# A second GpSimd drain near the end of the page stage, and two pages fewer turned on TensorE, in an attention and expert-routing kernel

## The chip, the cores and the metric

One core of one Trainium2 chip runs the whole program. The metric is the device time of an execution in microseconds (us). Several chips were used: times of one kernel on two of them differ by 1 to 2%, so only kernels timed on the same chip, in the same rounds, are compared.

## The reference, cut to what matters

The program computes random-feature attention over 8 batches, 8 heads, 576 positions, and sends its output through a mixture of 8 experts:

```python
x = attn_out.transpose(0, 2, 1, 3).reshape(B, S, H * D)     # 4608 tokens of 512
logits = x @ w_gate
e = argmax(logits) or the expert of the token before, by a local gate
h = maximum(x[b, s] @ w1[e], 0.0)                           # 512 -> 1024
out[b, s] = softmax(logits)[e] * (h @ w2[e])                # 1024 -> 512
```

The kernel sorts the tokens by expert into "pages" of 128 tokens, 18 pages for each half of the batch ("epoch 0" and "epoch 1") and 2 overflow pages that always run. A page is gathered from memory, turned (transposed), multiplied with its expert's first matrix, turned again, multiplied with the second, scaled, and scattered to the output rows.

## The kernel before: the parts that matter

NEP is 18. A page's step does three things: the hidden product of page j, the turning of the hidden tile of page j - 1, and the fetching ahead.

```python
NST = 2 * NEP + 2          # 38 pages
NT = NEP + 3               # pages below NT are turned on TensorE, the others by a DMA transpose

def page(j, nw, gates):
    def mid():                                   # between the two halves of the hidden product
        if j + 1 < NT:
            xts[j + 1] = turn_pe(xgs.pop(j + 1))         # 4 TensorE transposes and a ScalarE copy
    ...
    if j < NST:
        hs[j] = hidden(j, xts.pop(j), pages[j][1], mid)
    ...
    if j >= 1:
        h, ev = hs.pop(j - 1)                            # half of the tile by DMA once j >= NT
        done.append((pages[j - 1], hidden_t(h, FC // 2 if NT <= j < NST - 1 else FC), ev))
    ...
    if j + 5 < NST:
        gs = pages[j + 5][0]
        xgs[j + 5] = fetch(gs[-1:], xgs.get(j + 5))      # GpSimd gather, five pages ahead
    ...
    if NT <= j + 3 < NST:
        xts[j + 3] = turn(xgs.pop(j + 3))                # SyncE DMA transpose
    for _ in range(nw):
        w_load()                                         # GpSimd, plain transfers of weights
    if j == NEP + 6:
        nc.gpsimd.drain()
```

`nc.gpsimd.drain()` puts a DRAIN into GpSimd's list of instructions; the program's own ending, after the last page, has one too (the "closing drain"). Each page ends in `output`: eight TensorE matmuls, one VectorE product `y`, and a GpSimd scatter (`indirect_dma_start`). There are four buffers for `y`. Outputs lag behind, so the last ones follow each other without hidden products between them:

```python
while done:
    output(*done.pop(0), last=len(done) % 2 == 0)
```

The softmax here doesn't subtract the row's maximum and nothing guards it: scores larger than these inputs give would overflow.

## Time and profile before

| | before |
|---|---|
| median of the timed runs | 324.06 us (324.0 to 325.06) |
| span of the traced execution (a run of 319.12 us) | 317.3 us |
| page stage, TensorE without a gap | about 198 to 307 us |
| from the last product `y` to the end | about 9.4 us |

The run whose trace was kept was some 5 us faster than the timed ones. The lines that carry the argument stand in the prediction.

### The profile page before, as it was taken

Reading aid. Unit: us, or ns where it says so; the run is one execution under the profiler, and the core shown is the slowest. Engines: PE = TensorE matmul, PEld = TensorE weight load, DVE = VectorE, ACT = ScalarE, POOL = GpSimd, SP = SyncE. Lnnn points to the kernel's source line nnn. Section 1 sums busy time; section 2 is a strip of 40 time slices with the busy share of each in tenths; the row PEclk is TensorE's granted clock in tenths of the full one; section 3 lists DMA queues with packets and bytes.
Section 4 is the critical chain, followed back from the end, with each engine's and each line's share of the span. In section 5 each row is a group of like instructions: output and inputs, shape, how many; then the busy total and the mean of one; then the engine's idle time right before and its main releaser. Section 6 shows DMA issues by size and latency. Waiting matters only on the chain. (4 is left out here: it accounts for less than half of the span.)

```text
span 317.3 us, 8143 instructions
## 1 busy us (share of the span) xinstructions
PE 255.9 (81%) x2973; PEld 153.8 (48%) x2993; DVE 180.5 (57%) x406; ACT 152.5 (48%) x230; POOL 175.5 (55%) x264
## 2 busy tenths in 40 slices
PE   0276778787877765849989979999999999999970
PEld 0154555565555544525545647554444444445420
DVE  3478578978979878962556572433323343334430
ACT  1056798988989886625454545421222212212000
POOL 8459855655478743277666543065527767332550
PEclk9999999999999999556999999999999999999996
DMA  7999999999979999979999931146746866631330
GB/s 239 296 208 253 301 212 270 278 245 243 284 125 226 228 239 227 226 193 192 242 215 225 228 96 44 43 132 160 177 132 181 211 169 176 151 103 50 144 143 20
DMA packets 49386, 59.69 MB, mean 188 GB/s; under 512 B 22288, under 2 KB 31504, under 8 KB 49344
## 3 DMA queue, kind: packets, MB, share of 16 engines
q0 software_dynamic: 23088, 40.58, 60.2%
q1 hardware_dynamic: 22176, 13.77, 15.6%
q10 hardware_dynamic: 4080, 4.77, 4.6%
q8 instruction: 28, 0.46, 0.5%
q14 instruction: 14, 0.11, 0.1%
HBM read 67.16 MB, written 14.68 MB: 258 GB/s over the span
## 5 line engine op out<-in xcount | busy, mean ns | idle before, releaser
L604 PE MATMUL pj<-w_all,xt 128*128 x290 | 74.6, 385 | 2.6 <-DVE lg L297 1.4
L609 ACT ACTIVATE arena<-pj 128x1024 bf16<-128x1024 f32 x38 | 38.9, 1024 | 70.7 <-PE pj L604 68.0
L635 POOL DMA_INDIRECT out_dram<-y,idr x38 | 37.9, 998 | 52.2 <-DVE y L634 43.3
L218 POOL TENSOR_TENSOR va<-vs,ek 128x512 bf16<-128x512 f32 (+1 forms) x40 | 38.2, 958 | 34.1 <-ACT ek L209 33.9
L574 POOL DMA_INDIRECT xg<-x_tok,ix x36 | 37.6, 1044 | 27.4 <-PE tp L587 10.6
L200 DVE TENSOR_REDUCE kmx<-pj 128x8 f32<-128x1024 f32 x36 | 43.9, 1220 | 13.2 <-ACT kvb L237 10.1
L206 ACT ACTIVATE kp<-pj 128x1024 bf16<-128x1024 f32 x36 | 37.5, 1041 | 19.1 <-DVE kmx L200 19.1
L143 POOL DMA_DIRECT2D w_all<-in_moe_w_dram x64 | 35.8, 564 | 16.7 <-DMA w_all<-in_moe_w_dram 13.2
L604 PEld LDWEIGHTS <-xt 128*128 128x128 bf16 x304 | 28.7, 99 | 29.1 <-issue 1.7
L267 ACT ACTIVATE qp<-pj 128x1024 bf16<-128x1024 f32 x36 | 37.7, 1047 | 10.5 <-PE pj L261 10.5
L634 DVE TENSOR_SCALAR y<-po,prb 128x512 f32<-128x512 f32 x24 | 18.0, 750 | 28.1 <-PE po L629 26.8
L168 PE MATMUL tp<-ident_bf,ks 128*128 128x128 bf16 x128 | 13.5, 233 | 15.4 <-DMA ks<-in_k_dram 8.6
L619 DVE COPY ht<-tp 128x1024 bf16<-128x1024 bf16 (+1 forms) x20 | 12.2, 609 | 23.9 <-PE tp L616 23.9
L291 DVE TENSOR_TENSOR xr<-po,rd 128x512 bf16<-128x512 f32 x36 | 24.9, 691 | 1.2
L194 PE MATMUL pj<-om_bd,kt 128*128 128x256 bf16 x144 | 23.4, 288 | 2.5 <-ACT kp L206 0.7
L589 ACT COPY xt<-tp 128x512 bf16<-128x512 bf16 x21 | 12.3, 585 | 25.5 <-PE tp L587 24.3
L629 PE MATMUL po<-w_all,ht 128*128 x100 | 24.2, 379 | 0.2
L629 PEld LDWEIGHTS <-ht 128*128 128x128 bf16 x160 | 15.2, 98 | 16.0
L619 DVE COPY arena<-tp 128x512 bf16<-128x512 bf16 (+1 forms) x18 | 9.8, 543 | 22.9 <-PE tp L616 22.9
L716 ACT COPY qt<-tp 128x512 bf16<-128x512 bf16 x36 | 21.8, 607 | 1.2 <-DVE kt L714 1.0
L629 PEld LDWEIGHTS <-arena 128*128 128x128 bf16 x144 | 13.7, 98 | 14.9
L629 PE MATMUL po<-w_all,arena 128*128 x87 | 20.7, 379 | 0.1
(154 smaller groups left out, 375.5 us busy)
## 6 DMA issues: line engine op xcount, KB each, us to landing
w_all<-in_moe_w_dram POOLq DMA_DIRECT2D x64, 256.0 KB, 10.5
vs<-in_v_dram SPq DMA_DIRECT2D x8, 1152.0 KB, 11.9
arena<-in_q_dram POOLq DMA_DIRECT2D x4, 1152.0 KB, 19.3
x_tok<-xr ACTq DMA_DIRECT2D x16, 256.0 KB, 6.1
ks<-in_k_dram POOLq DMA_DIRECT2D x7, 576.0 KB, 16.7
out_dram<-y,idr POOLq DMA_INDIRECT x38, 2.8
xg<-x_tok,ix POOLq DMA_INDIRECT x36, 3.9
x_tok<-xr ACTq DMA_DIRECT2D x4, 128.0 KB
```

Of the source, the lines that this page charges most:

```text
L143: nc.gpsimd.dma_start(out=wdst[l][:, ds(e * WE + i * 1024, 1024)].rearrange("p (c f) -> p c f", f=w), in_=src[e].rearrange(("(c p) f -> p ...
L194: nc.tensor.matmul(pj[:, 2 * i:2 * i + 2, :].rearrange("p a d -> p (a d)"), lhsT=kts[t][:, i], rhs=om_bd, start=True, stop=True)
L200: nc.vector.tensor_reduce(mx, kpj[t], axis=AX, op=Alu.max)
L206: nc.scalar.activation(kp, kpj.pop(t), Act.Exp, scale=scale)
L218: nc.gpsimd.tensor_tensor(va[:, x:x + 4 * n, 0:Dh].rearrange("p (h r) d -> p h r d", h=4), stg[P, "v", g].rearrange("p h (r d) -> p h r d" ...
L267: nc.scalar.activation(qp, qpj.pop(s), Act.Exp, scale=scale)
L291: nc.vector.tensor_tensor(xrs[s][:, u % 2, :].rearrange("p (g h d) -> p g h d", g=2, h=4), ov[:, :, :, 0:Dh], rd.to_broadcast([128, 2, 4, ...
L574: nc.gpsimd.indirect_dma_start(out=xg, out_offset=None, in_=src, in_offset=bass.IndirectOffsetOnAxis(ap=ix, axis=0), bounds_check=TE - 1, ...
L604: nc.tensor.matmul(h_ps[:, c, :], lhsT=xt[:, dc, :], rhs=w1_all[:, ds(ev + (dc * F + c * 512), 512)], start=(dc == 0), stop=(dc == DC - 1))
L609: nc.scalar.activation(h, h_ps.rearrange("p a x -> p (a x)").rearrange("p (c f) -> p f c", f=FC), Act.Relu)
L629: nc.tensor.matmul(y_ps[:, 0, :], lhsT=htn[0][:, f], rhs=w2_all[:, ds(ev + f * D, D)], start=(f == 0), stop=(f == FC - 1))
L635: s_ = nc.gpsimd.indirect_dma_start(out=out_flat, out_offset=bass.IndirectOffsetOnAxis(ap=idr[:, c:c + 1], axis=0), in_=y, in_offset=None, ...
```

## The change

The intent: fewer transposes on TensorE, which sets the pace of the page stage, and a shorter closing drain, by draining GpSimd once more while it has time.

```diff
-    NT = NEP + 3
+    NT = NEP + 1
...
-        if j == NEP + 6:
+        if j in (NEP + 6, NST - 1):
 
             nc.gpsimd.drain()
```

## The prediction

> **What bounds the kernel now.** I read four views of the kernel before: the page's slices, the busy time of each engine by stretches, the timeline of the page stage by engine, and last the single-line views of the drains. The chain of waits is of no use here: it covers only the last two pieces, from 308.42 us on, because everything before is one gapless engine and everything after is no counted work.
>
> The windows give the stages. Columns are stretch, length, then busy us of each engine, clock, DMA share and GB/s:
>
> ```profile
> 150.00:186.00 36.00, 32.81 (x303) 20.65 (x307) 21.93 (x74) 18.81 (x24) 22.32 (x32) 1.00 1.03 214
> 186.00:198.00 12.00, 11.43 (x93) 7.79 (x95) 5.29 (x16) 6.42 (x8) 4.85 (x5) 1.00 0.20 56
> 198.00:203.00 5.00, 4.95 (x43) 2.98 (x42) 2.03 (x6) 2.48 (x5) 0.00 (x0) 1.00 0.23 52
> 203.00:287.00 84.00, 83.53 (x445) 40.62 (x452) 29.68 (x50) 19.78 (x20) 43.66 (x43) 1.00 0.59 155
> 287.00:307.00 20.00, 19.89 (x104) 9.42 (x103) 8.80 (x12) 1.02 (x1) 9.40 (x10) 1.00 0.27 106
> 309.50:317.30 7.80, 0.00 (x0) 0.00 (x0) 0.00 (x0) 0.00 (x0) 0.00 (x0) 0.63 0.06 20
> ```
>
> From 198 to 307 us TensorE (first busy column) is busy 108.4 of 109 us; VectorE, ScalarE and GpSimd stay near or under half. So in this stage every microsecond taken off TensorE's list comes off the end, and nothing else does. After 309.5 no engine computes, yet the core runs on for 7.8 us. That tail is pure serial waiting, the second place where time can be saved. The drains show what it is made of (columns: line, engine, operation, count, shortest/median/longest ns, first and last start):
>
> ```profile
> L690 POOLq DRAIN  x1: 6862/6862/6862, 230.5 to 230.5; - x1
> ...
> L814 POOLq EVENT_SEMAPHORE  x4: 17/43/2684, 309.3 to 312.2; - x4
> L814 POOLq INC_SWDGE_SEM  x1: 970/970/970, 312.2 to 312.2; - x1
> ...
> L848 POOLq DRAIN  x3: 51/103/3234, 313.2 to 317.0; - x3
> L848 SPq DRAIN  x3: 7/7/13, 313.9 to 316.7; - x3
> ```
>
> Read in order: the last scatter is issued at 308.18, GpSimd waits 2.68 us for it to land (to about 312.2), spends 0.97 us on an increment, and then its closing drain takes 3.23 us (313.2 to 316.5) with nothing left in flight; 0.8 us of barriers follow. The drain of SyncE takes 7 to 13 ns, so the 3.23 us is GpSimd's own.
>
> **What the Trainium skill says.** "VectorE: DVE Perf Modes", section "The DRAIN you can't avoid", says that the boilerplate drains of a kernel's ends take about 12 ns on all five engines. The trace agrees for SyncE (7 to 13 ns) and for two of GpSimd's three at the end (51 and 103 ns, order of size), but not for GpSimd's first one behind 39 transfers (3234 ns); no page I found gives its price. "Perfetto Trace Analysis", section "Sequencer-only Instruction (DRAIN, etc)", says the record is the execution alone, without its semaphore wait. The mid-page drain's record (230.5 to 237.4) nevertheless overlaps a gather of the same engine that ran at 231.44 to 232.49, so it includes waiting for the engine's own queue. "DMA: Bandwidth & Descriptors", section "SWDGE vs HWDGE vs iDMA", says that GpSimd's cores write the descriptors of their transfers into rings; a drain that has rings to tidy would cost by the number of transfers since the last one, which is my reading and not the page's. "TensorE: Matmul & The Clock Gate", section "Part 4: PE-mode transpose", puts a 128x128 bf16 transpose at about 275 ns in a kernel; the trace's pitch is much shorter, see below, and I use that.
>
> **The change, part 1: fewer transposes on TensorE.** The bound NT goes from 21 to 19. It sets which pages are turned on TensorE and where only half of a hidden tile is. The instruction order of the changed kernel confirms it: pages 19 and 20 lose four transposes each, the hidden tiles handled at steps 19 and 20 lose four of eight each, two ScalarE copies go, two VectorE copies become half as wide, and SyncE gets four more DMA transposes. 16 TensorE transposes go in all. Their price is the step from one group's start to the next one's on the timeline (columns: start, length, engine, line, operation):
>
> ```profile
> 201.40 0.38 PE L587 MATMUL tp<-ident_bf,xg 128*128 128x128 bf16 x4
> 201.62 1.03 PE L604 MATMUL pj<-w_all,xt 128*128 x4
> ...
> 206.63 0.61 PE L616 MATMUL tp<-ident_bf,arena 128*128 128x128 bf16 x8
> 207.07 1.89 PE L629 MATMUL po<-w_all,arena 128*128 x8
> ...
> 216.15 0.39 PE L616 MATMUL tp<-ident_bf,arena 128*128 128x128 bf16 x4
> 216.38 0.38 PE L629 MATMUL po<-w_all,arena 128*128 x1
> ```
>
> Four page transposes take 201.62 - 201.40 = 0.22 us of pitch, not the 0.38 of the length column, because successive groups overlap. Eight hidden transposes take 0.44, four take 0.23: so a halved tile gives 0.21. Sum: 2 x 0.22 + 2 x 0.21 = **0.86 us**, all of it after 201.4, inside the gapless stretch, so I let it reach the end whole.
>
> What is added for it lies beside other work. The page transposes by DMA took 2.5 to 4.5 us to land; those of pages 19 and 20 are issued at steps 16 and 17, about 195 to 199 us, and read by the hidden matmuls at 204.65 and 210.53 less part 1: 5 us or more in hand, in a stretch where the DMA engines are 20 to 23% busy. The halves of hidden tiles are read some 16 pages later.
>
> **Part 2: the second drain, seen from the end.** It stands in GpSimd's list at step 37 of 38. Ten scatters follow it (two of step 37, eight after; the ten from 292.20 to 308.18 on the timeline), where the closing drain now has 29 scatters and 10 gathers, 39 transfers, behind the first one. If the closing drain costs by transfers, with the empty drains of 0.05 and 0.10 us as its floor, it is (3.23 - 0.1) / 39 = 80 ns each, and becomes 0.1 + 10 x 0.08 = 0.9 us: a gain of **2.3 us**. The mid-page drain warns against that slope: it had 116 transfers behind it (77 plain, 30 gathers, 9 scatters) and, counted from the end of the gather before it, took 237.38 - 232.49 = 4.89 us, not 9. Two readings fit both: a cap (4.89 / 0.08 = about 61 transfers that can be outstanding), or a fixed part. A straight line through (39, 3.23) and (116, 4.89) has 21.6 ns each on 2.39 us; then 10 transfers cost 2.6 us and the gain is **0.6 us**.
>
> **Part 2, seen from where it stands.** The new drain has to wait for the scatter of 288.30, which is through at 289.28, earlier by part 1: about 288.4. It has 29 transfers behind it: 2.4 us by the first slope, 3.0 by the line, at most the 4.9 of the first. The first drain was followed by its next scatter 0.86 us later (237.38 to 238.24), so that scatter starts at 291.7 to 294.2 against 291.3 without the drain. Behind the first drain the scatters caught up at one per 1.31 us. Nine such intervals are 11.8 us and the present ones sum to 15.98 (308.18 - 292.20): 4.2 us of slack, against a delay of 0.4 to 2.9. The last scatter is not delayed. The four output buffers hold for the same reason: TensorE ran on without a gap while the first drain held GpSimd for longer.
>
> **Rivals.**
> First, the closing drain has a price that hardly depends on what is behind it. For: 116 transfers cost only 1.5 times as much as 39. Against: the two empty ones cost 0.05 and 0.10 us, so something behind it must matter. Then only part 1 counts: 324.06 - 0.9 = 323.2.
> Second, the price goes by transfers up to a cap. For: the empty drains, and that someone kept the first drain. Then 324.06 - 0.9 - 2.3 = 320.9.
> Third, the new drain holds the scatters up to the end, by waiting for the landing of the scatter before it and then working 4 us or more: the last scatter would come up to 1 us late, eating part 1; the time would be 323 to 324. Against: the 4.2 us of slack.
> Fourth, part 1 is hidden: the DMA transposes of pages 19 and 20 come late because SyncE's list is in order and one of them must wait for a buffer or a hidden tile. TensorE would then show a wait at the hidden matmuls near 204 and 210. In the trace before, the same pattern from page 21 on leaves no gap in 203 to 287 (83.5 of 84 us busy), so I give it 1 in 20.
>
> **Time, range, chances.** I weigh the drain's gain: about half for 2.3, a third for 0.6, the rest for nothing: 0.5 x 2.3 + 0.33 x 0.6 = 1.35 us. With part 1: 324.06 - 0.86 - 1.35 = **321.8 us**. The range runs from the full slope with a little over (320.4) to nearly no gain from the drain (323.4); the three runs before lie within 1.1 us, which I leave room for. Faster by over 2% would need 317.6 or less: the whole closing drain and both parts together give 0.86 + 3.2 = 4.1 us, 320.0, so there is nothing in the change to reach it: 0.02. Slower by over 2% needs 330.5, a stall of 6 us that nothing here suggests, unless a run falls in another state of the clock: 0.01. Within 2%: 0.97.
>
> **What would show it.** Part 1: 19 ScalarE copies of turned pages instead of 21, 19 page transposes on SyncE instead of 17, TensorE still gapless from 198, and the last product's multiplication on VectorE at about 306.3 instead of 307.15. Part 2: two drains at line 690; the second's record starts near 284 and spans its wait for the scatter before it; the gaps between the last ten scatters shrink to 0.3 us and are back at 0.74 before the last. The closing drain: about 0.9 us by the proportional reading, 2.6 by the line, 3.2 by the first rival; this one number decides most of the result. The prediction is wrong if the closing drain is not shorter, if the last scatter is still catching up, or if TensorE shows idle time before the hidden matmuls of pages 19 or 20.

## The result, and the profile after

The changed kernel took 320.44 us in the median (320.01 to 321.17, 4 runs) against 324.56 (324.0 to 325.39, 4 runs). The ratio is 0.9873, interval 0.984 to 0.9907; it is the mean of one kernel's fast runs over the mean of the other's of the same rounds, so not quite the ratio of the medians. That is 4.1 us or 1.3% less: within the band of 2%, inside the forecast range, 0.04 us above its lower end.

The drains of the changed kernel, in the same columns as in the prediction:

```profile
L690 POOLq DRAIN  x2: 4056/5460/6864, 233.1 to 292.7; - x2
...
L814 POOLq EVENT_SEMAPHORE  x4: 17/43/2546, 313.9 to 316.6; - x4
L814 POOLq INC_SWDGE_SEM  x1: 400/400/400, 316.7 to 316.7; - x1
...
L848 POOLq DRAIN  x3: 51/103/861, 317.1 to 318.6; - x3
```

The closing drain fell from 3234 to 861 ns. The increment just ahead of it, which the forecast took as fixed, fell from 970 to 400 ns. Both are on the serial tail.

But the traced span is 318.8 us, longer than the 317.3 of the trace before, while the timed runs say the opposite. Two things pull the traces apart. One lies ahead of everything that was changed. These are the granted TensorE clock in 40 slices, before and then after:

```profile
PEclk9999999999999999556999999999999999999996
```
```profile
PEclk9999899999999979756999999999999999999998
```

The mean granted clock is 0.959 in both, but the slices with a lowered clock (5 to 8) lie elsewhere. The rectifier of page 0 (ScalarE's maximum with 0, one for each page) starts 3.3 us later in the second trace (149.3 against 146.0 us), though the edits stand behind it. The other lies in the page stage. Busy time of TensorE (first busy column) after the change, of 84 us:

```profile
203.00:287.00 84.00, 82.26 (x443) 39.81 (x442) 28.03 (x50) 19.88 (x20) 41.58 (x41) 1.00 0.62 152
```

TensorE has a hole of some 1.7 us between 203 and 287. It waits there for VectorE, which is late, shown here on the timeline (start, length, engine, line, operation, and in brackets the idle time before it):

```profile
246.60 0.42 DVE L619 COPY ht<-tp 128x512 bf16<-128x512 bf16 x1 [1.42 <-PE tp L616]
251.10 0.75 DVE L634 TENSOR_SCALAR y<-po,prb 128x512 f32<-128x512 f32 x1 [4.08 <-PE pj L629]
251.77 0.74 DVE L634 TENSOR_SCALAR y<-pj,prb 128x512 f32<-128x512 f32 x1
```

The product at 251.10 comes 3 us later than its place in the pattern, and its follower runs directly behind it. The same happens at 259.6 and 271.0. Whether this belongs to the change had to be tested.

### The profile page after: what moved, and what is told of

Same layout as the page of the kernel before. It is cut to its first block, busy times and chain, and to the rows that moved or that the text cites. A ratio compares the mean times of both kernels' runs of the same rounds, so it can differ in the third digit from the quotient of the medians.

```text
span 318.8 us, 8136 instructions
## 1 busy us (share of the span) xinstructions
PE 257.5 (81%) x2977; PEld 153.7 (48%) x2977; DVE 179.9 (56%) x406; ACT 151.0 (47%) x228; POOL 175.1 (55%) x264
## 5 line engine op out<-in xcount | busy, mean ns | idle before, releaser
L604 PE MATMUL pj<-w_all,xt 128*128 x304 | 76.4, 385 | 3.6 <-DVE lt L294 3.4
L589 ACT COPY xt<-tp 128x512 bf16<-128x512 bf16 x19 | 11.1, 584 | 25.3 <-PE tp L587 22.0
```

The source lines that it names most:

```text
L604: nc.tensor.matmul(h_ps[:, c, :], lhsT=xt[:, dc, :], rhs=w1_all[:, ds(ev + (dc * F + c * 512), 512)], start=(dc == 0), stop=(dc == DC - 1))
```

## The experiments

Eleven runs gave correct results and one was wrong on purpose. The first eight were on one chip, called A; the last four on another, called B. The kernel before had a median of 319.5 to 319.6 us on A and 324.6 on B.

### The two parts alone, and both kernels again (chip A)

The second drain alone:

```diff
-        if j == NEP + 6:
+        if j in (NEP + 6, NST - 1):
```

> The second drain alone, turns as before. Theory A (the closing drain costs about 80 ns for each transfer since the last drain): closing drain 0.86 us as in the whole change, against 3.23 before; the increment ahead of it 0.4 against 0.97 us; gain 2.4 to 3.0 us, three quarters of the whole gain of about 4 us. Rival B (the closing drain is short only because the transposes left): closing drain stays near 3.2 us, gain under 0.5 us.

Measured: 317.09 us, ratio 0.9923 (0.989 to 0.9956), which is 2.5 us faster (here and below, gains in us are worked out from the ratio; the medians differ by 2.4). The closing drain was 861 ns, the increment 400 ns.

The turns alone:

```diff
-    NT = NEP + 3
+    NT = NEP + 1
```

> Two turned pages and two half tiles off TensorE, one drain as before. Theory A: gain 0.86 us (16 transposes at their pitch), closing drain 3.23 us still. Rival B: closing drain drops. Rival C (the turns are worth more than their pitch, because they also free a wait in the gate stage): gain 1.5 to 2 us, and with it the 1.9 us by which the whole change beat the forecast.

Measured: 319.05 us, ratio 0.9976 (0.9946 to 1.0006), 0.8 us faster, not clear of zero by its interval. Its trace shows what the page stage gained better. From the rectifier of page 16 to that of page 37 took 92.05 us in both traces of the kernel before and 91.15 us here: 0.90 us less. The closing drain stayed at 3234 ns. So rival B falls: transposes on SyncE's list do nothing for GpSimd's drain. In the page stage the turns are worth their pitch. Rival C has nothing for it in the trace (from page 0 to page 16 it took 50.78 us, and 50.82 in the second trace of the kernel before), though the interval of the timing alone reaches 1.7 us.

The changed kernel, unedited, once more:

> The whole change once more, for the sum on this chip and a second trace. If the parts add: gain equal to drain_only plus turns_only, about 3.3 to 4.1 us; closing drain 0.86 us. The first trace had VectorE late by 2 to 4 us at three products after the first drain; if that is of one execution, it is gone here; if it belongs to the change, it is here again at the same products.

Measured: 316.62 us, ratio 0.9893 (0.9859 to 0.9927), 3.4 us faster. The parts add, as far as intervals of about 1 us either way can tell: 2.5 + 0.8 = 3.3 by the ratios, 2.4 + 0.5 = 2.9 by the medians, which give 2.9 for both together too. The late products are gone, as the timeline of the same place shows:

```profile
245.58 0.42 DVE L619 COPY ht<-tp 128x512 bf16<-128x512 bf16 x1 [1.20 <-PE tp L616]
247.31 0.75 DVE L634 TENSOR_SCALAR y<-po,prb 128x512 f32<-128x512 f32 x1 [1.30 <-remote]
```

The product follows its copy by 1.30 us as everywhere, and TensorE is busy 83.53 of 84 us again. So the change does not bring the late products with it; what does is taken up under chip B.

The kernel before, unedited, a single look for a second trace:

> The kernel before, for a second trace: its first trace (span 317.3 us, run 319.1) was some 5 us faster than its timed runs (324.0 to 325.4). Expected: a run near 324, span near 322, with the first of the page stage some us later than in the first trace; closing drain 3.23 us and the increment 0.97 us if these belong to the kernel and not to the execution.

Measured: one run of 319.62 us, span 317.8, no different from the other runs before on this chip. My expectation of a run near 324 was wrong: the first trace looks like one from a chip of this kind, and not like an odd execution. The closing drain was 3234 ns and the increment 970 ns to the nanosecond, so these belong to the kernel.

This pair from one chip lets the spans be added up. From 317.8 to 315.6 us: closing drain -2.37, increment -0.57, turns -0.90, wait for the last scatter to land 2.70 to 2.11, thus -0.59 (2.1 to 2.8 in all traces whose last scatters come in time and have whole rows, without an order that follows the kernels), and a page stage that began 2.15 us later. The sum is -2.28, against -2.2 measured. The places that the change meant to shorten are the first three: 3.84 us, which lies inside the intervals of both measured gains (4.1 and 3.4 us).

The later start of the page stage was first taken for an accident. But every trace with the turns moved has it: on A, page 0's rectifier starts at 147.8 to 148.8 us in those four, and at 146.0 to 146.8 in the five others (the first trace of the kernel before counted with A). About 1.8 us is lost between some 119 and 126 us, in the attention, where ScalarE does the same work in the same order in all of them. The granted clock of that stretch was 0.50 in the four and 0.97 to 1.00 in the five. In the slices it is the sixteenth digit, second trace of the kernel before and then the turns alone:

```profile
PEclk9999999999999959757999999999999999999995
```
```profile
PEclk9999999999999965767999999999999999999995
```

That is more than the 0.90 us that the turns save later on, and the span of the turns alone is 317.8 us, as long as that of the kernel before. Whether the changed program brings this on or these executions had it by chance was not tested. So the turns are shown to shorten the page stage, and not shown to shorten the kernel.

### What a drain costs, and whether it has a cap (chip A)

The kernel before without its drain:

```diff
         if j == NEP + 6:
 
-            nc.gpsimd.drain()
+            pass
```

> The kernel before without its one drain amid the pages: 155 transfers lie behind the closing drain. Theory A with a cap (80 ns a transfer, about 60 outstanding at most): closing drain about 4.9 us, 1.6 to 2 us slower than before. Theory A without a cap: 12.7 us, 9 to 10 us slower. Rival (a fixed part of 2.4 us and 22 ns a transfer): 5.7 us, 2.5 us slower.

Measured: 326.26 us, ratio 1.0197 (1.0158 to 1.0236), 6.3 us slower.

```profile
L814 POOLq INC_SWDGE_SEM  x1: 2150/2150/2150, 312.9 to 312.9; - x1
```
```profile
L848 POOLq DRAIN  x3: 51/103/8069, 315.0 to 323.7; - x3
```

8.07 us for the drain: neither the capped 4.9, nor the uncapped 12.7, nor the 5.7 of the straight line. All my readings were wrong in the same place, for they gave one price to every transfer. With two prices all numbers agree. The closing drains behind 10 and 39 transfers, all indirect (gathers and scatters), give (3234 - 861) / 29 = 81.8 ns each on 0.04 us. Behind the 8.07 us lie 78 indirect ones, 6.38 us, which leaves 1.65 us for the 77 plain loads, 21 ns each. This second price is fitted, so the next line is its test. The drain amid the pages then has 39 x 0.0818 + 77 x 0.0214 + 0.04 = 4.88 us; its net time was 4.89. So what transfers cost simply adds up, with no cap up to 155 of them and no fixed part to speak of. Why a plain transfer is cheaper (by its kind, or because part of its work was done earlier) these runs do not tell.

The drain at the late place alone:

```diff
-        if j == NEP + 6:
+        if j == NST - 1:
```

> One drain alone, at the place of the second, with 145 transfers behind it. Theory A: closing drain 0.86 us, so as fast as drain_only (0.75% faster than before), if the late drain itself stays short enough to be caught up. With a cap it works about 4.9 us and the last scatter is in time or under 1 us late; without a cap it works 11.9 us, the last ten scatters come some 7 us late, and the kernel is 4 to 5 us slower than before.

Measured: 317.95 us, ratio 0.9938 (0.9901 to 0.9975), 2.0 us faster than before, and by its ratio 0.5 us slower than with both drains (timed in other rounds, and the intervals overlap). The closing drain was 866 ns. The late drain had 145 transfers behind it; the two prices say 8.07 - 0.82 = 7.25 us, and it worked 7.26 (from the end of the scatter at 288.97 to the end of its record). This shows what happens when a drain is too long for its place. VectorE, then TensorE:

```profile
297.47 0.75 DVE L634 TENSOR_SCALAR y<-pj,prb 128x512 f32<-128x512 f32 x1 [0.97 <-PE pj L629]
300.90 0.75 DVE L634 TENSOR_SCALAR y<-po,prb 128x512 f32<-128x512 f32 x1 [2.68 <-PE pj L629]
302.18 0.75 DVE L634 TENSOR_SCALAR y<-pj,prb 128x512 f32<-128x512 f32 x1 [0.53 <-DMA out_dram<-y,idr]
```
```profile
301.70 1.89 PE L629 MATMUL po<-w_all,arena 128*128 x8 [0.82 <-DVE y L634]
```

The four output buffers are full of rows waiting to be scattered; VectorE waits for a scatter to land, and TensorE then waits for VectorE. That costs about 1 us at the end (the last ten products take 16.96 us from the start of the first to that of the last, against 15.99 in the kernel before). The first drain thus pays twice: it takes work from the closing drain, and it makes the second one short enough for its place.

### A third drain, and the last page of epoch 1 (chips A and B)

A third drain with four scatters left, on top of the change:

```diff
     while done:
         output(*done.pop(0), last=len(done) % 2 == 0)
+        if len(done) == 4:
+            nc.gpsimd.drain()
```

> The whole change plus a third drain when four scatters are left. Theory A: closing drain 0.04 + 4 x 0.082 = 0.37 us, the increment ahead of it shorter too (0.2 to 0.3 us); the third drain's own cost (6 transfers, 0.5 us and a gap) is caught up by the last scatter; 0.5 to 0.7 us faster than the whole change. Rival: a fixed floor of some 0.8 us is reached at ten transfers, and nothing is gained; or the last scatter comes late and it is slower.

Measured on A: 316.24 us, ratio 0.9889 (0.9856 to 0.9922); not told apart from the change (0.9893). The price list held: the closing drain was 371 ns for four transfers, the increment 280. The place failed. GpSimd at the end:

```profile
302.65 0.98 POOL L635 DMA_INDIRECT out_dram<-y,idr  x1 [0.75 <-DVE y L634]
306.53 0.98 POOL L635 DMA_INDIRECT out_dram<-y,idr  x1 [2.90 <-DVE y L634]
307.82 0.98 POOL L635 DMA_INDIRECT out_dram<-y,idr  x1 [0.30 <-DVE y L634]
309.11 0.98 POOL L635 DMA_INDIRECT out_dram<-y,idr  x1 [0.31 <-issue]
310.40 0.99 POOL L635 DMA_INDIRECT out_dram<-y,idr  x1 [0.30 <-issue]
```

```profile
L811 POOLq DRAIN  x1: 3250/3250/3250, 302.4 to 302.4; - x1
```

The drain ended at 302.4 + 3.25 = 305.7, 2.0 us after the scatter ahead of it had left GpSimd, though six transfers should cost 0.5. That is about the time that scatter needed to land, so the drain seems to have waited for the transfer in flight (by the match of the times; nothing in the trace names the wait). The last scatter, with no gap above 0.31 us ahead of it, is still catching up: it comes 0.85 us later behind its product than in the change, and itself waits 3.7 us to land, right behind the others. That takes back the 0.6 us won.

The same with six scatters left:

```diff
+        if len(done) == 6:
+            nc.gpsimd.drain()
```

> The whole change plus a third drain with six scatters left instead of four. A drain late in the list waits about 2.7 us for the scatter ahead of it to land (the third drain with four left worked 2.0 us for 6 transfers, not 0.5), then 0.3 and 0.86 us to the next scatter: 2.1 us behind, caught up at 0.43 us a scatter, which five scatters just do. Closing drain 0.04 + 6 x 0.082 = 0.53 us, increment 0.32; last scatter at most 0.2 us late; 0.3 to 0.4 us faster than the whole change. Rival: it is not caught up and nothing is gained.

Measured on B: 320.37 us, ratio 0.987 (0.9827 to 0.9914). The closing drain was 534 ns and the increment 320, as expected, and the last scatter was in time (1.03 us behind its product, as before the change). The 0.4 us this wins by the trace is too small for the timing: the change beside it had 320.41.

No page of epoch 1 on TensorE:

```diff
-    NT = NEP + 1
+    NT = NEP
```

> The whole change with no page of epoch 1 turned on TensorE: the bound NT one lower still. By the pitch, 8 transposes fewer, 0.45 us faster than the whole change. Rival: page 18's gather lands too late for a DMA turn issued at step 15, TensorE waits at its hidden matmuls, and it is the same or slower; the author kept this page on TensorE.

Measured on A: 316.27 us, ratio 0.9898 (0.9862 to 0.9934). By the trace pages 16 to 37 took 90.53 us, 0.62 less than with the change, and TensorE had no new wait there; by the timing it is not told apart. The rival (a late gather) is not seen.

Both together:

```diff
-    NT = NEP + 1
+    NT = NEP
...
+        if len(done) == 6:
+            nc.gpsimd.drain()
```

> No page of epoch 1 on TensorE, and the third drain with six scatters left. By the sum of the traces: 0.65 us from the turns and 0.3 to 0.4 us from the drain, so about 1 us (0.3%) faster than the whole change, 1.3 to 1.5% faster than before. Rival: lost in the 0.35% of the interval.

Measured on B: 320.28 us, ratio 0.9868 (0.9823 to 0.9912). The rival is right: lost in the interval.

The change, unedited, beside these:

> The whole change on the same chip, as the measure for the two above: about 1.1% faster than before, closing drain 0.86 us.

Measured on B: 320.41 us, ratio 0.9856 (0.9809 to 0.9903), 4.7 us faster by the ratio. So no version that beats the change was shown, though two have shorter traced parts.

The late products are back in this trace, at the same places as in the first one:

```profile
246.42 0.42 DVE L619 COPY ht<-tp 128x512 bf16<-128x512 bf16 x1 [1.42 <-PE tp L616]
250.79 0.75 DVE L634 TENSOR_SCALAR y<-po,prb 128x512 f32<-128x512 f32 x1 [3.95 <-PE pj L629]
```

All four traces from B have them and none of the eight from A, with the same kernel on both. They go with the chip (or its surroundings), not with the change. The recording is a rival here: the files of these traces, and of the first trace of the change, hold 3896 to 3957 records of semaphore updates, all others 4860 to 4962. What VectorE waited for in the first trace was TensorE: its product starts 0.02 us after an update of TensorE's semaphore at 251.08 us, 3.0 us after the (modelled) end of the matmuls before it. Why that update is late is open. No trace of the kernel before from B was taken, so whether it loses more there, and whether that is why the measured gain is 4.1 to 4.7 us with those times and 3.4 on A, stays open; the intervals overlap, so there may be nothing to explain.

### By transfer or by row (chip B, a single look)

The last ten scatters write half their rows; the result is wrong.

```diff
+        r_ = 64 if len(outs) >= 28 else 128
-            ... ap=idr[:, c:c + 1], axis=0), in_=y, ...
+            ... ap=idr[0:r_, c:c + 1], axis=0), in_=y[0:r_], ...
```

> The last ten scatters write 64 rows each instead of 128 (a wrong result on purpose): half the descriptors in as many transfers. If the drain's price goes by transfers, the closing drain stays at 0.86 us and the increment at 0.40. If it goes by descriptors or rows, the closing drain is about 0.45 us.

Measured: one run of 322.47 us.

```profile
L849 POOLq DRAIN  x3: 51/103/861, 318.8 to 320.2; - x3
```

861 ns again, and the increment 400: for scatters the price goes by the transfer, not by its rows.

## Why the prediction was right or wrong

**What bounds the kernel: right for the tail, half shown for TensorE.** Work taken off the serial tail came off the end (2.5 us). Work taken off TensorE came off the page stage (0.90 us), with TensorE still gapless there. The forecast let it "reach the end whole", and that is not shown: 0.8 us by the ratio with an interval that holds zero, and in its trace none, because the page stage began later.

**Part 1: right in the page stage, and nearly to size.** Forecast 0.86 us, traced 0.90. One sign failed with the later start: the last product begins at 308.9 us in the second trace of the change and at 311.8 in the first, not at 306.3. The counts came as said; the first DMA-turned page of the changed kernel shows no transposes between its hidden matmuls and half a hidden tile behind them (second trace of the change):

```profile
207.11 1.89 PE L604 MATMUL pj<-w_all,xt 128*128 x7
208.83 0.39 PE L616 MATMUL tp<-ident_bf,arena 128*128 128x128 bf16 x4
209.06 1.89 PE L629 MATMUL po<-w_all,arena 128*128 x8
```

**Part 2, the closing drain: the proportional reading was right, the weighing of it was not.** The sentence "I weigh the drain's gain: about half for 2.3, a third for 0.6, the rest for nothing" is the step that cost the most: the gain is 2.37 us, so the term of 1.35 was 1.0 us short. The doubt came from the drain amid the pages, about which I wrote "Two readings fit both: a cap ... or a fixed part". The kernel without its drain ruled out both. A third, two kinds of transfer with two prices, fits (4.88 against 4.89 us); that it is the kind and not the age of a transfer that sets the price is not shown. The composition of the 116 transfers (77 plain, 30 gathers, 9 scatters) stood in the forecast and was not used.

**A term left out.** The tail's increment was listed at 0.97 us and then treated as fixed. It goes by the transfers too: 280, 320, 400 and 970 ns behind 4, 6, 10 and 39 indirect ones, 20 ns each on 0.2 us (the 2150 ns without the drain leave 5 ns for a plain one, again about a quarter). That is another 0.57 us. With the two terms right the forecast would have been 324.06 - 0.86 - 2.37 - 0.57 = 320.3 us, against 320.44 measured. As it stood it was 1.6 us short in these two terms, so that the result still fell inside the range, by 0.04 us, is luck. It also corrects the statement that the whole change could give at most 4.1 us; that bound held only because the drain did not vanish.

**Part 2, the place: right in the result, short in the mechanism.** The second drain worked 2.84 us net, where the proportional price says 2.42, and the next scatter came 0.86 us after its end, 3.71 us idle in all. The scatter ahead had landed 2.6 us after its issue at 290.06, that is 1.6 us after it left GpSimd, so that this wait and the price in full do not add up to 2.84 either; how the two combine stays open:

```profile
290.06 0.98 POOL L635 DMA_INDIRECT out_dram<-y,idr  x1 [2.69 <-DVE y L634]
294.74 0.98 POOL L635 DMA_INDIRECT out_dram<-y,idr  x1 [3.71 <-issue]
296.03 0.98 POOL L635 DMA_INDIRECT out_dram<-y,idr  x1 [0.30 <-DVE ht L619]
...
309.94 0.98 POOL L635 DMA_INDIRECT out_dram<-y,idr  x1 [0.75 <-DVE y L634]
```

By the last scatter the gap is back at 0.75, so nothing was late. Two signs of the forecast were off: the drain's record began at 289.8 us, just ahead of that scatter, and not near 284, and only one gap shrank to 0.3. The third rival, that the drain waits for a landing and delays the end, was perhaps right about the wait and wrong about the end in this kernel; in the late drain alone and in the third drain with four scatters left it came true.

**The first rival (a price that does not depend on what is behind) and the fourth (part 1 hidden)** both fell: 371, 534, 861, 3234 and 8069 ns, and no wait at the turned pages.

## What to carry to other kernels

The tail after the last computation is serial and worth a list of its own: here each gather or scatter since the last GpSimd drain cost about 0.1 us there, 82 ns in the closing drain and 20 ns in the increment ahead of it. Drain GpSimd earlier, where it has slack, but leave enough transfers behind the drain to catch up: a drain worked up to 1.5 us longer than its transfers cost, it seems because it waited for the scatter in flight, and when the scatters fall behind by more than the output buffers hold, TensorE stops. When one duration does not fit a price per piece, split the pieces by kind before inventing a cap or a fixed part. And follow a gain to the end of the trace: 0.90 us won in one stage can be lost in another.

## What the Trainium skill lacked or had wrong

- No page gives the price of a GpSimd drain by the transfers issued since the last one: 0.37, 0.53, 0.86 and 3.23 us behind 4, 6, 10 and 39 indirect transfers (82 ns each), 8.07 us behind 78 indirect and 77 plain ones (which leaves 21 ns for a plain one). It did not change when ten scatters had half their rows.
- "VectorE: DVE Perf Modes", section "The DRAIN you can't avoid", has the drains of a kernel's ends at about 12 ns on all five engines. SyncE's were 7 to 13 ns, GpSimd's 51 and 103 ns and the first of its three 371 to 8069 ns.
- "Perfetto Trace Analysis", section "Sequencer-only Instruction (DRAIN, etc)", has the record as the execution alone, without the semaphore wait. It does not tell of time inside the record that belongs to work ahead: a GpSimd drain's record began at 302.4 us, before the scatter ahead of it ran (302.65), and lasted 3.25 us for six transfers worth 0.5.
- No page that I found tells of the increment ahead of the closing drain: 280 to 2150 ns, by the number of transfers.
- "TensorE: Matmul & The Clock Gate", section "Part 4: PE-mode transpose", has about 275 ns for a 128x128 transpose in a kernel, which is the length of one; it gives no pitch. In a row of eight the pitch was 55 ns (0.44 us), and 16 of them taken away gave 0.90 us.
